# Score matmuls of an attention layer in quarters of the TensorE array, two rounds at a time

## The chip, the cores and the metric

One core of a Trainium2 chip runs the kernel; the other seven have nothing to do. The metric is the time of one execution on the device, in microseconds (us). Instructions run on TensorE (matmuls, PE in the rows; its weight loads PEld), VectorE (DVE), ScalarE (ACT) and GpSimd (POOL); SyncE (SP) issues most of the DMAs.

## What is computed

An attention layer with a causal window of 128 positions and a distance bias, over 4 batches of 8 heads of 64 with 576 positions, and behind it two feed-forward layers over its 2304 tokens:

```python
scores = scale * np.matmul(q, k.transpose(0, 1, 3, 2))
bias = slopes[:, None, None] * (-np.abs(rel).astype(np.float32))[None, :, :]
mask = (rel >= 0) & (rel < window)
scores = np.where(mask, scores + bias[None], -1000000000.0)
...
attn = attn / (np.sum(attn, axis=-1, keepdims=True) + 1e-09)
out = np.matmul(attn, v)
...
x = ((x @ w_a) * (x @ w_b)) @ w_out      # 512 -> 1536 -> 512
return bent(x @ w_in2) @ w_out2          # 512 -> 2048 -> 512
```

The weights are 64-bit floats; the kernel turns each slice of 128 columns or rows into a high and a low 32-bit part ("decodes" it) before it is used.

## The kernel before

**Attention.** Two heads are worked on together, as a pair `hp`: their 64 dimensions each fill the 128 partitions. A batch has nine blocks of 64 queries; each sees its own 64 keys and the 128 before, so that a block of scores has up to 192 columns (64 and 128 for the first two). Two blocks are a round (`m`, five rounds for batches 1 to 3, the last with one block). A unit is a batch, a pair of heads and a part of the rounds; batch 0 has eight units in two parts, the other batches four each.

`scores` (L315) works on a round. One matmul a block (L327) gives the 64 queries of both heads at once: its left operand is a block of `diag`, 128x128, that holds q of the first head in the upper left quarter, q of the second in the lower right, and zeros elsewhere. q and k of batches 1 to 3 come in from DMA as 32x32 pieces and are transposed by VectorE in `prep_unit` (L300, two half transposes of q into the diagonal of `diag`; L303, k). Scores and bias are added by VectorE, which takes the maximum in the same pass (L333), ScalarE does the exponential (L337), GpSimd and VectorE the reciprocal of the sum (L342, L343), and GpSimd and ScalarE the scaling (L346, L348). Three rounds later `transposes` turns the probabilities by matmuls with the identity (L359), a copy brings them back, and five rounds later `values` multiplies them with v (L391), a unit at a time, with 64x64 and 128x64 tiles; the product goes to a pair `xh`, `xl` (L153, L147). All matmuls of attention are of plain 32-bit floats, and each leaves two records in the trace, a transposing one leaves one.

PSUM: `ps_at` has four banks for scores (one per round), transposes (one) and value products (two).

**Feed-forward.** `gate` and `down1` run up and down products (L540 to L542, then L613, L641 to L643 and L679 to L681) with high and low parts in three matmuls each. The first 1536 tokens are taken in half blocks of 256 as soon as their attention is done; these run interleaved with attention, a step of attention after every one or two steps of products (`PACE`). The first half block needs twelve decoded weights one after the other, the second finds them there. Decoding takes five or six VectorE passes over 128x512 (L491 to L499), GpSimd's sums (L505, L147) and ScalarE's copies (L489, L506).

**Order.** The Python code emits instructions in this interleaved order; a scheduler with a model of the engines then sets the order on each engine, which is fixed in the program. Each engine runs its list strictly in that order, waiting on semaphores.

Of the kernel before, what the change touches and what calls it, by code (L numbers as in the profile page):

```python
# [9 lines left out]
F32 = mybir.dt.float32  # L10
# [4 lines left out]
ALU = mybir.AluOpType  # L15
# [11 lines left out]
def attention_and_two_ffns(  # L27
# [59 lines left out]
    SB = 4  # L87
# [82 lines left out]

    biases = []
    for hp in range(NPAIR):
        bias = att.tile([P, 3 * D], F32, tag=f"bias{hp}", name=f"bias{hp}", bufs=1)
        for j in range(2):
            nc.vector.tensor_scalar(
                bias[j * D : (j + 1) * D], rel[j * D : (j + 1) * D],
                -(2.0 ** (-8.0 * (2 * hp + j + 1) / H)) / QSCALE, NEG / QSCALE,
                ALU.mult, ALU.max,
            )
        biases.append(bias)  # L180
    diag = []
    for z in range(NDIAG):
        t = att.tile([P, NQ, P], F32, tag=f"diag{z}", name=f"diag{z}", bufs=1)
        nc.vector.memset(t, 0.0)
        diag.append(t)

# [100 lines left out]
    def prep_unit(u):  # L287
        b, part, hp = units[u]
        if b == 0:
            turn_start(part, hp, diag[u % NDIAG])  # L290
            if (part, hp) == (1, NPAIR - 1):
                retired.update(("first", z) for z in range(5))
            return
        q0, q1, k0 = PART[part]
        qr, kr = prep[b, part, hp]
        qd = diag[u % NDIAG]
        kt = att.tile([P, NK], F32, tag="kt", name="kt")
        for j in range(2):
            me = slice(j * D, (j + 1) * D)
            nc.vector.transpose(  # L300
                qd[me, : (q1 - q0) // D, me], qr[me].rearrange("p (n t) -> p n t", t=D)
            )
        nc.vector.transpose(kt[:, : q1 - k0], kr)  # L303
        prep[b, part, hp] = (qd, kt)

    def qblocks(m):
        return [i for i in (2 * m, 2 * m + 1) if i < S // D]
# [4 lines left out]
    rounds = {}  # L312
    values_of = {}

    def scores(b, hp, m):  # L315
        part = part_of(b, m)
        q0, _, k0 = PART[part]
        qd, kt = prep[b, part, hp]
        ps = ps_at.tile([P, 2, 4 * D], F32, tag="at", name="ps_s")
        count["t"] += 1  # L320
        s_sb = probs[count["t"] % SB]
        at = lambda z, i: s_sb[:, z, first_col(i) :]
        nmax = att.tile([P, 2], F32, tag="nmax", name="nmax", bufs=6)
        ssum = att.tile([P, 2], F32, tag="ssum", name="ssum", bufs=6)
        for z, i in enumerate(qblocks(m)):
            c = first_col(i)
            nc.tensor.matmul(  # L327
                ps[:, z, c : 3 * D], qd[:, i - q0 // D, :],
                kt[:, (i - 2) * D + c - k0 : (i + 1) * D - k0], start=True, stop=True,
            )  # L330
        for z, i in enumerate(qblocks(m)):
            cs = slice(first_col(i), 3 * D)
            nc.vector.tensor_tensor_reduce(  # L333
                at(z, i), ps[:, z, cs], biases[hp][:, cs], -QSCALE, BIG,
                ALU.add, ALU.min, nmax[:, z : z + 1],
            )
            nc.scalar.activation(  # L337
                at(z, i), at(z, i), AF.Exp,
                bias=nmax[:, z : z + 1], scale=-1.0, accum_out=ssum[:, z : z + 1],
            )  # L340
        n = len(qblocks(m))
        nc.gpsimd.tensor_scalar(ssum[:, :n], ssum[:, :n], 1e-9, 1.0, ALU.add, ALU.mult)  # L342
        nc.vector.reciprocal(ssum[:, :n], ssum[:, :n])  # L343
        for z, i in enumerate(qblocks(m)):
            if E_N[2 * b + (m >= 2)][z] == "A":
                nc.scalar.activation(at(z, i), at(z, i), AF.Copy, scale=ssum[:, z : z + 1])  # L346
                continue
            ENG[E_N[2 * b + (m >= 2)][z]].tensor_scalar(  # L348
                at(z, i), at(z, i), ssum[:, z : z + 1], 1.0, ALU.mult, ALU.mult
            )  # L350
        rounds[b, hp, m] = s_sb
# [12 lines left out]
    def values(b, hp, part):  # L364

        q0, _, _ = PART[part]
        vt = values_of[b, part, hp]
        ms = ROUNDS_OF[part]  # L370
        pts = {m: rounds.pop((b, hp, m)) for m in ms}
        po = [ps_at.tile([P, TB], F32, tag="at", name="ps_o") for _ in range(2)]
        todo_ = []
        for m in ms:
            todo_ += [(0, m, slice(0, D), vt, m, 1, j) for j in range(2)]
            if m > 0 and len(qblocks(m)) == 2:
                todo_ += [(1, m, slice(D, P), vt, m - 1, 1, j) for j in range(2)]
        for m in ms:
            if m > 0:
                todo_ += [(0, m, slice(0, P), vt, m - 1, 0, j) for j in range(2)]  # L380
            if len(qblocks(m)) == 2:
                todo_ += [(1, m, slice(0, P), vt, m, 2, j) for j in range(2)]
        seen = set()
        left = {}
        for z, m, _, _, _, _, j in todo_:
            left[z, m, j] = left.get((z, m, j), 0) + 1
        for z, m, rows, vt, n, u, j in todo_:
            me = slice(j * D, (j + 1) * D)
            left[z, m, j] -= 1
            c = (m - ms[0]) * D  # L390
            nc.tensor.matmul(  # L391
                po[z][me, c : c + D], vt(n, j)[rows], pts[m][rows, u, me],
                start=(z, j) not in seen, stop=left[z, m, j] == 0, skip_group_check=True,
            )
            seen.add((z, j))
        for z in range(2):
            mine = [m for m in ms if z < len(qblocks(m))]
            tok = lambda m: b * S + (2 * m + z) * D
            for i in sorted({tok(m) // TB for m in mine}):
                those = [m for m in mine if tok(m) // TB == i]  # L400
                c, n0 = (those[0] - ms[0]) * D, (tok(those[0]) - blocks[i][0]) // D
                src = po[z][:, c : c + len(those) * D].rearrange("p (n t) -> p n t", t=D)
                xh, xl = (
                    x[:, hp].rearrange("p (n t) -> p n t", t=D)[:, n0 : n0 + 2 * len(those) - 1 : 2]
                    for x in xs[i]
                )
                ecopy(E_X[2 * b + int(part == 1)], xh, src)
                minus(nc.vector, xl, src, xh)
# [7 lines left out]
    ]  # L416
    done = set()

    def attention():
        load_start()  # L420
        prep_unit(0)
        seen = -1
        for n in range(len(todo) + LV):
            if n < len(todo):
                u, t = todo[n]
                if u != seen:
                    seen = u
                    if u + 1 < len(units):
                        prep_unit(u + 1)
                    if u + AHEAD < len(units):  # L430
                        load_unit(*units[u + AHEAD])
                    values_of[units[u]] = load_values(*units[u])
                scores(*t)
                yield
            if 0 <= n - LT < len(todo):
                transposes(*todo[n - LT][1])
# [367 lines left out]
```

## Time and profile before

| | |
|---|---|
| median of 3 runs | 995.21 us (995.11 to 998.65) |
| the profiled execution | 996.27 us |
| its span, first to last instruction | 994.4 us |
| mean granted TensorE clock | 0.992 of full |
| busy: TensorE matmuls, weight loads | 969.7, 842.4 us |
| busy: VectorE, ScalarE, GpSimd | 609.7, 407.2, 177.7 us |

Busy time of TensorE counts every moment at which a matmul is under way; matmuls overlap, so the sum of their lengths is longer, and the step from one start to the next says more than a length. Shares over the whole span are averages over stages with different limits, so the trace is read by windows below.

### The profile page before, as it was taken

How to read it: one execution, taken by the hardware profiler on the slowest of the kernel's cores; microseconds unless marked ns; L12 is line 12 of the kernel's file. 1: busy time of each engine (PE TensorE's matmuls, PEld its weight loads, DVE VectorE, ACT ScalarE, POOL GpSimd, SP SyncE). 2: the span in 40 equal slices, each digit the busy share in tenths (PEclk: the TensorE clock that was granted, in tenths of full speed). 3: DMA queues.
4: the chain of work that ended last, by engine and by line, in shares of the span. 5: the costliest groups of instructions: out<-in, count | busy, mean ns of one | idle time of the engine just before them, and what ended most of it. 6: DMA issues, size and time to landing. Idle time of an engine off the chain costs nothing.

```text
span 994.4 us, 15931 instructions
## 1 busy us (share of the span) xinstructions
PE 969.7 (98%) x6052; PEld 842.4 (85%) x6052; DVE 609.7 (61%) x1366; ACT 407.2 (41%) x998; POOL 177.7 (18%) x285
## 2 busy tenths in 40 slices
PE   5997999999999999999999999999999999999998
PEld 4876999999989888888988888888888888888887
DVE  6699855553616993223995299635995446644443
ACT  5887677663214441112342245333552223322222
POOL 5567633331101100000212224000020000000001
PEclk9999999999999999999999999999999999999999
DMA  9756444213311331000331023100230000001111
GB/s 208 146 122 147 110 87 74 57 35 133 113 53 45 125 106 43 0 1 1 105 91 60 1 63 85 44 1 1 85 107 22 1 1 21 1 1 43 43 43 63
DMA packets 115403, 61.83 MB, mean 62 GB/s; under 512 B 87040, under 2 KB 107520, under 8 KB 114944
## 3 DMA queue, kind: packets, MB, share of 16 engines
q1 hardware_dynamic: 113184, 60.31, 22.7%
q8 instruction: 47, 0.77, 0.3%
q10 hardware_dynamic: 2144, 0.52, 0.2%
q14 instruction: 28, 0.23, 0.1%
HBM read 52.95 MB, written 7.86 MB: 61 GB/s over the span
## 4 chain that ended last, share of the span: by engine, by line
PE 87%; DVE 3%; DMA 1%; issue 1%; ACT 0%; POOL 0%; DVEq 0%; POOLq 0%; SPq 0%; ACTq 0%
PE mm L540 16%; PE mm L541 16%; PE mm L542 16%; PE acc L681 7%; PE acc L679 7%; PE acc L680 7%; PE acc L613 4%; PE acc L643 3%; PE acc L642 3%; PE acc L641 3%; PE ps_s L327 3%; PE ps_o L391 2%; PE ps_t L359 1%; DMA w<-in_moe_w_out_dram 1%; DVE e L499 0%
## 5 line engine op out<-in xcount | busy, mean ns | idle before, releaser
L540 PE MATMUL mm<-xh,wh 128*128 128x512 f32 (+1 forms) x912 | 318.6, 350 | 0.0
L541 PE MATMUL mm<-xl,wh 128*128 128x512 f32 (+1 forms) x912 | 315.6, 346 | 0.0
L542 PE MATMUL mm<-xh,wl 128*128 128x512 f32 (+1 forms) x912 | 315.0, 346 | 0.1
L540 PEld LDWEIGHTS mm<-xh,wh 128*128 128x128 f32 x912 | 173.0, 190 | 21.6
L541 PEld LDWEIGHTS mm<-xl,wh 128*128 128x128 f32 x912 | 173.1, 190 | 21.1
L542 PEld LDWEIGHTS mm<-xh,wl 128*128 128x128 f32 x912 | 172.8, 189 | 21.3 <-POOL wl L147 0.4
L596 ACT ACTIVATE c_sb<-c_sb,half 128x512 f32<-128x512 f32 (+1 forms) x80 | 54.5, 681 | 165.6 <-DVE c_sb L595 165.6
L585 DVE TENSOR_TENSOR a_sb<-mm,a_sb 128x256 f32<-128x256 f32 (+1 forms) x74 | 40.1, 542 | 121.1 <-PE mm L542 114.0
L679 PE MATMUL acc<-wh,gh 128*128 128x512 f32 x288 | 112.3, 390 | 0.2 <-ACT gh L562 0.2
L680 PE MATMUL acc<-wl,gh 128*128 128x512 f32 x288 | 112.2, 389 | 0.0
L681 PE MATMUL acc<-wh,gl 128*128 128x512 f32 x288 | 110.4, 390 | 0.3 <-POOL gl L147 0.3
L595 DVE TENSOR_SCALAR c_sb<-mm 128x512 f32<-128x512 f32 (+1 forms) x80 | 50.8, 636 | 81.9 <-PE mm L542 79.0
L147 POOL TENSOR_TENSOR gl<-c_sb,gh 128x256 fp32r<-128x256 f32 x16 | 15.6, 974 | 384.1 <-ACT gh L562 374.2
L147 POOL TENSOR_TENSOR gl<-a_sb,gh 128x256 fp32r<-128x256 f32 x40 | 35.4, 886 | 255.6 <-ACT gh L562 255.0
L597 DVE SCALAR_TENSOR_TENSOR c_sb<-mm,c_sb 128x512 f32<-128x512 f32 (+1 forms) x80 | 50.7, 635 | 39.0 <-ACT c_sb L596 39.0
L580 ACT COPY a_sb<-mm 128x256 f32<-128x256 f32 (+1 forms) x74 | 34.4, 464 | 89.2 <-PE mm L542 89.0
L562 ACT CAST gh<-a_sb 128x256 fp32r<-128x256 f32 (+1 forms) x74 | 37.2, 503 | 82.0 <-DVE a_sb L585 81.7
L562 ACT CAST gh<-c_sb 128x512 fp32r<-128x512 f32 (+1 forms) x80 | 46.2, 579 | 55.9 <-DVE c_sb L597 47.7
L506 ACT CAST wh<-e 128x512 fp32r<-128x512 f32 x68 | 42.2, 621 | 63.1 <-DVE e L505 38.2
L489 ACT ACTIVATE e<-w 128x512 f32<-128x512 f32 x65 | 43.8, 673 | 56.8 <-DVE wl L147 13.9
L642 PE MATMUL acc<-gl,wh 128*128 128x512 f32 (+1 forms) x184 | 66.3, 362 | 0.2 <-DVE gl L147 0.2
L337 ACT ACTIVATE s<-s,nmax 128x192 f32<-128x192 f32 (+2 forms) x144 | 62.0, 433 | 9.9 <-DVE nmax L333 9.5
(77 smaller groups left out, 1614.8 us busy)
## 6 DMA issues: line engine op xcount, KB each, us to landing
w<-in_moe_w_out_dram SPq DMA_DIRECT2D x28, 512.0 KB, 3.6
w<-in_moe_w_in_dram SPq DMA_DIRECT2D x16, 512.0 KB, 3.6
w<-in_moe_w_a_dram SPq DMA_DIRECT2D x12, 512.0 KB, 3.8
w<-in_moe_w_b_dram SPq DMA_DIRECT2D x12, 512.0 KB, 3.7
out_dram<-osum SPq DMA_DIRECT2D x18, 256.0 KB, 2.1
qraw<-in_q_dram SPq DMA_DIRECT2D x48, 72.0 KB, 2.8
kraw<-in_k_dram SPq DMA_DIRECT2D x48, 72.0 KB, 2.8
v<-in_v_dram SPq DMA_DIRECT2D x25, 128.0 KB, 2.8
```

The source lines that it names most:

```text
L147: eng.tensor_tensor(out_, a, hi.bitcast(F32), ALU.subtract)
L337: nc.scalar.activation(at(z, i), at(z, i), AF.Exp, bias=nmax[:, z : z + 1], scale=-1.0, accum_out=ssum[:, z : z + 1],)
L540: nc.tensor.matmul(ps, wh[:, cs], xh[:, c], start=(c == 0), stop=False)
L541: nc.tensor.matmul(ps, wh[:, cs], xl[:, c], start=False, stop=False)
L542: nc.tensor.matmul(ps, wl[:, cs], xh[:, c], start=False, stop=(c == NC - 1))
L562: nc.scalar.copy(hi[:, :n], t[:, :n])
L595: nc.vector.tensor_scalar(c_sb[:, :n], ph[:, :n], -1.0, None, ALU.max)
L596: nc.scalar.activation(c_sb[:, :n], c_sb[:, :n], AF.Square, bias=half, scale=0.5)
L642: nc.tensor.matmul(accs[c][:, :n], wh[:, cs], gl, start=False, stop=False)
L679: nc.tensor.matmul(accs[s], gh[:, ss], wh, start=begin, stop=False)
L680: nc.tensor.matmul(accs[s], gh[:, ss], wl, start=False, stop=False)
L681: nc.tensor.matmul(accs[s], gl[:, ss], wh, start=False, stop=end)
```

## The change

For batches 1 to 3 `diag` and its zeros go. q is transposed like k, in one pass over 128 partitions, into `qt`. `scores_two` takes two rounds that follow each other (also from one unit into the next) and two banks. A block becomes two matmuls of 64 rows by 64 columns of the array, one per head: head j's q and k lie on partitions 64j and up, so it uses row half j; the first block of a round writes to bank 0 with head j at partitions 64j, the second to bank 1 with the heads swapped. So the four matmuls of a round use four different quarters of the array. VectorE and ScalarE work on the two rounds one after the other as before; the bias has a second copy with the heads swapped, and `values` reads the turned probabilities from the other half. The next unit is prepared behind the scores that open a unit, not ahead of them. Batch 0 keeps `diag`, which is now five blocks long instead of nine.

```diff
-        bias = att.tile([P, 3 * D], F32, tag=f"bias{hp}", name=f"bias{hp}", bufs=1)
+        bias = att.tile([P, 2, 3 * D], F32, tag=f"bias{hp}", name=f"bias{hp}", bufs=1)
+        for y in range(2):
+            for j in range(2):
+                me = slice((j ^ y) * D, ((j ^ y) + 1) * D)
+                nc.vector.tensor_scalar(
+                    bias[me, y], rel[me],
...
-        t = att.tile([P, NQ, P], F32, tag=f"diag{z}", name=f"diag{z}", bufs=1)
+        t = att.tile([P, NQ - 4, P], F32, tag=f"diag{z}", name=f"diag{z}", bufs=1)
...
-        for j in range(2):
-            me = slice(j * D, (j + 1) * D)
-            nc.vector.transpose(
-                qd[me, : (q1 - q0) // D, me], qr[me].rearrange("p (n t) -> p n t", t=D)
-            )
+        nc.vector.transpose(qt[:, : q1 - q0], qr)
         nc.vector.transpose(kt[:, : q1 - k0], kr)
...
+    def scores_two(two):
+        banks = [ps_at.tile([P, 2, 4 * D], F32, tag="at", name="ps_s") for _ in range(2)]
+        for y, (b, hp, m) in enumerate(two):
+            qt, kt = prep[b, 2, hp]
+            for z, i in enumerate(qblocks(m)):
+                c = first_col(i)
+                for j in range(2):
+                    me, to = (slice(h * D, (h + 1) * D) for h in (j, j ^ z))
+                    nc.tensor.matmul(
+                        banks[z][to, y, c : 3 * D], qt[me, i * D : (i + 1) * D],
+                        kt[me, (i - 2) * D + c : (i + 1) * D], start=True, stop=True,
+                        skip_group_check=True,
+                    )
+        return [[bank[:, y] for bank in banks] for y in range(2)]
...
-                at(z, i), ps[:, z, cs], biases[hp][:, cs], -QSCALE, BIG,
+                at(z, i), ps[z][:, cs], biases[hp][:, z if b else 0, cs], -QSCALE, BIG,
...
+            turned = slice((j ^ z) * D, ((j ^ z) + 1) * D) if b else me
...
-                po[z][me, c : c + D], vt(n, j)[rows], pts[m][rows, u, me],
+                po[z][me, c : c + D], vt(n, j)[rows], pts[m][rows, u, turned],
...
-                scores(*t)
+                if t[0] == 0:
+                    if u != seen:
+                        begin(u)
+                        seen = u
+                    scores(*t, scores_one(*t))
+                else:
+                    if n % 2 == 0:
+                        banks = scores_two([r for _, r in todo[n : n + 2]])
+                    scores(*t, banks[n % 2])
+                    if u != seen and (n % 2 or todo[n + 1][0] == u):
+                        begin(u)
+                        seen = u
```

The order that the scheduler makes of it differs, on TensorE above all. In the rows a name is a tile with its number, `mm` and `acc` are products of the feed-forward layers, `ps_s`, `ps_t`, `ps_o` scores, transposes and value products, and the size is that of the output. First, two wide rounds of the first pair of heads of batch 2 on TensorE, before:

```order
L542 MATMUL mm_1923<-xh0_106,wl_1161 128x256
L327 MATMUL ps_s_1898<-kt_1650,diag0_128 128x192 x2
L359 MATMUL ps_t_1917<-ident_84,s3_138 128x128 x3
L327 MATMUL ps_s_1927<-kt_1650,diag0_128 128x192 x2
L359 MATMUL ps_t_1943<-ident_84,s0_132 128x128 x2
L540 MATMUL mm_1969<-xh0_106,wh_1254 128x256
```

and after the change:

```order
L575 MATMUL mm_2172<-xh1_108,wl_243 128x256
L339 MATMUL ps_s_1975<-kt_1701,qt_1700 64x192 x2
L339 MATMUL ps_s_1976<-kt_1701,qt_1700 64x192 x2
L339 MATMUL ps_s_1975<-kt_1701,qt_1700 64x192 x2
L339 MATMUL ps_s_1976<-kt_1701,qt_1700 64x192 x2
L380 MATMUL ps_t_1998<-ident_84,s0_140 128x128 x2
```

Two rounds with a bank each, four matmuls on the whole array, became one stretch of eight on quarters, with tiles of another shape in front of it and behind it.

Second, two wide rounds of the next pair of heads on TensorE, after the change:

```order
L413 MATMUL ps_o_2061<-pt_1969,v2_150 64x64 x2
L380 MATMUL ps_t_2143<-ident_84,s3_146 128x128 x3
L339 MATMUL ps_s_2152<-kt_1916,qt_1915 64x192 x4
L573 MATMUL mm_2172<-xh1_108,wh_242 128x256
L573 MATMUL mm_2203<-xh1_108,wh_293 128x256
L574 MATMUL mm_2172<-xl1_109,wh_242 128x256
L575 MATMUL mm_2172<-xh1_108,wl_243 128x256
L574 MATMUL mm_2203<-xl1_109,wh_293 128x256
L575 MATMUL mm_2203<-xh1_108,wl_294 128x256
L339 MATMUL ps_s_2153<-kt_1916,qt_1915 64x192 x4
L380 MATMUL ps_t_2176<-ident_84,s0_140 128x128 x3
```

Here the four matmuls on bank 0 (`ps_s_2152`) and the four on bank 1 (`ps_s_2153`) stand apart, with six products on the whole array between them.

Third, VectorE between its last passes on two weights (`w64_1143` is the ninth, `w64_1158` the tenth that is decoded), before:

```order
L499 SCALAR_TENSOR_TENSOR e_1147<-w64_1143,e_1147 128x512
L333 ISA s1_134,nmax_1337<-ps_s_1336,bias1_119 128x192
L333 ISA nmax_1337 128x1
L333 ISA s1_134,nmax_1337<-ps_s_1336,bias1_119 128x192
L333 ISA nmax_1337 128x1
L343 RECIPROCAL ssum_1281<-ssum_1281 128x2
L585 TENSOR_TENSOR a_sb_1022<-mm_1024,a_sb_1022 128x256
L492 TENSOR_SCALAR e_1162<-e_1162 128x512
L333 ISA s2_136,nmax_1362<-ps_s_1361,bias1_119 128x192
L333 ISA nmax_1362 128x1
L300 STREAM_TRANSPOSE diag1_130<-qraw_1223 64x9x64 x2
L303 STREAM_TRANSPOSE kt_1427<-kraw_1228 128x576
```

and the stretch behind the ninth weight's last pass after the change:

```order
L532 SCALAR_TENSOR_TENSOR e_1169<-w64_1165,e_1169 128x512
L147 TENSOR_TENSOR xl1_109<-ps_o_1207,xh1_108 128x64
L354 ISA s3_146,nmax_1308<-ps_s_1299,bias1_121 128x192
L354 ISA nmax_1308 128x1
L525 TENSOR_SCALAR e_1184<-e_1184 128x512
L528 TENSOR_SCALAR e_1184<-e_1184 128x512
L618 TENSOR_TENSOR a_sb_1034<-mm_1036,a_sb_1034 128x256
L354 ISA s0_140,nmax_1338<-ps_s_1298,bias1_121 128x192
L354 ISA nmax_1338 128x1
L529 SCALAR_TENSOR_TENSOR up_1185<-w64_1180,e_1184 128x512
```

The transposes of q and k that stood between the two weights are not there; the next ones (one of q, one of k) follow behind the tenth weight's last pass.

## Rows read from the trace of the kernel before

**Rows 1.** The page, busy time of each engine, share of the span, instructions:

```profile
PE 969.7 (98%) x6052; PEld 842.4 (85%) x6052; DVE 609.7 (61%) x1366; ACT 407.2 (41%) x998; POOL 177.7 (18%) x285
```

**Rows 2.** Windows: busy us (instructions) of each engine, granted clock, DMA share, GB/s:

```profile
25.40:50.00 24.60, 24.09 (x245) 21.24 (x246) 16.83 (x67) 21.54 (x76) 13.09 (x25) 0.93 0.73 143
50.00:99.70 49.70, 42.32 (x451) 36.17 (x451) 48.66 (x155) 39.51 (x135) 36.35 (x56) 0.95 0.64 135
99.70:102.50 2.80, 2.80 (x19) 2.61 (x18) 1.65 (x2) 0.26 (x1) 1.39 (x1) 0.63 0.73 118
102.50:227.10 124.60, 124.60 (x1434) 121.59 (x1432) 75.60 (x307) 86.66 (x313) 50.19 (x114) 1.00 0.31 70
```

**Rows 3.** Timeline of VectorE, 88 to 96 us: start, length, line, operation, tiles:

```profile
88.84 0.35 DVE L333 CUSTOM_DVE_ANT_0 s<-ps_s,bias 128x192 f32<-128x192 f32 x1
...
89.12 0.21 DVE L147 TENSOR_TENSOR xl<-ps_o,xh 128x64 fp32r<-128x64 f32 x1
89.25 1.53 DVE L496 SCALAR_TENSOR_TENSOR up<-w,e 128x512 uint32<-128x512 uint32 x1
...
92.22 0.68 DVE L499 SCALAR_TENSOR_TENSOR e<-w,e 128x512 f32<-128x512 uint32 x1
...
93.33 0.77 DVE L300 STREAM_TRANSPOSE diag<-qraw 64x576 f32<-64x576 f32 x1
94.03 0.56 DVE L492 TENSOR_SCALAR e<-e 128x512 f32<-128x512 f32 x1
```

**Rows 4.** Timeline of TensorE, 92 to 103.5 us; in brackets the idle time before:

```profile
94.93 0.47 PE L359 MATMUL ps_t<-ident,s 128*128 128x128 f32 x1 [2.47 <-POOL s L348]
...
99.69 0.41 PE L540 MATMUL mm<-xh,wh 128*128 128x256 f32 x1
...
102.51 0.71 PE L327 MATMUL ps_s<-kt,diag 128*128 128x64 f32 x4
102.98 0.36 PE L542 MATMUL mm<-xh,wl 128*128 128x256 f32 x1
```

**Rows 5.** Timeline of TensorE, 137 to 139 us:

```profile
137.15 0.81 PE L327 MATMUL ps_s<-kt,diag 128*128 128x192 f32 x4
137.80 0.49 PE L359 MATMUL ps_t<-ident,s 128*128 128x128 f32 x3
```

**Rows 6.** Groups by line and shape, TensorE: count, busy us, mean ns of one:

```profile
L327 PE MATMUL ps_s<-kt,diag 128*128 128x192 f32 x224 | 50.5, 344 | 2.2 <-DVE nmax L333 1.4 <-DVE xl L147 0.9
L327 PE MATMUL ps_s<-kt,diag 128*128 128x64 f32 x32 | 6.7, 295 | 1.2 <-DVE kt L155 0.8 <-DVE xl L147 0.4
```

**Rows 7.** Windows of L391 alone: matmuls, weight loads, clock, DMA:

```profile
131.59:132.32 0.73, 0.73 (x32) 0.66 (x33) 1.00 0.00 0
132.32:133.40 1.08, 1.08 (x36) 1.01 (x32) 1.00 0.30 56
```

**Rows 8.** Timeline of TensorE, 116.6 to 117.6 us:

```profile
116.68 0.28 PE L541 MATMUL mm<-xl,wh 128*128 128x256 f32 x1
116.80 0.28 PE L542 MATMUL mm<-xh,wl 128*128 128x256 f32 x1
117.01 0.32 PE L391 MATMUL ps_o<-pt,v 64*64 64x64 f32 x2
117.26 0.39 PE L613 MATMUL acc<-gh,wh 128*128 128x256 f32 x1
117.49 0.28 PE L613 MATMUL acc<-gl,wh 128*128 128x256 f32 x1
```

**Rows 9.** Groups by line, VectorE, to 240 us:

```profile
L300 DVE STREAM_TRANSPOSE diag<-qraw 64x576 f32<-64x576 f32 x24 | 18.5, 770 | 0.4
...
L184 DVE MEMSET diag<- 128x1152 f32 x2 | 2.0, 1018 | 0.4 <-issue 0.4
...
L175 DVE TENSOR_SCALAR bias<-rel 64x192 f32<-64x192 f32 x8 | 1.8, 252 | 0.0
```

**Rows 10.** Timeline of SP's queue, 0 to 60 us:

```profile
23.29 4.33 SPq L254 DMA_DIRECT2D qraw<-in_q_dram  x4
```

More of the change, by code (lines that the diff above doesn't have):

```diff
@@ L172, in attention_and_two_ffns @@
     for hp in range(NPAIR):
-        bias = att.tile([P, 3 * D], F32, tag=f"bias{hp}", name=f"bias{hp}", bufs=1)
-        for j in range(2):
[L175 to L178, printed above, removed]
-            )
+        bias = att.tile([P, 2, 3 * D], F32, tag=f"bias{hp}", name=f"bias{hp}", bufs=1)
[4 more added lines that the diff above has]
+                    bias[me, y], rel[me],
+                    -(2.0 ** (-8.0 * (2 * hp + j + 1) / H)) / QSCALE, NEG / QSCALE,
+                    ALU.mult, ALU.max,
+                )
         biases.append(bias)
@@ L295, in prep_unit @@
         qr, kr = prep[b, part, hp]
-        qd = diag[u % NDIAG]
+        qt = att.tile([P, NK], F32, tag="qt", name="qt")
         kt = att.tile([P, NK], F32, tag="kt", name="kt")
-        for j in range(2):
-            me = slice(j * D, (j + 1) * D)
-            nc.vector.transpose(
-                qd[me, : (q1 - q0) // D, me], qr[me].rearrange("p (n t) -> p n t", t=D)
-            )
+        nc.vector.transpose(qt[:, : q1 - q0], qr)
         nc.vector.transpose(kt[:, : q1 - k0], kr)
-        prep[b, part, hp] = (qd, kt)
+        prep[b, part, hp] = (qt, kt)
     def qblocks(m):
@@ L313, in attention_and_two_ffns, with scores_one @@
     values_of = {}
-    def scores(b, hp, m):
+    def scores_one(b, hp, m):
         part = part_of(b, m)
@@ L319, in scores @@
         ps = ps_at.tile([P, 2, 4 * D], F32, tag="at", name="ps_s")
[L320 to L324, printed above, removed]
         for z, i in enumerate(qblocks(m)):
@@ L330, in scores @@
             )
+        return [ps[:, z] for z in range(2)]
+    def scores_two(two):
[10 more added lines that the diff above has]
+                        skip_group_check=True,
+                    )
+        return [[bank[:, y] for bank in banks] for y in range(2)]
+    def scores(b, hp, m, ps):
+        count["t"] += 1
+        s_sb = probs[count["t"] % SB]
+        at = lambda z, i: s_sb[:, z, first_col(i) :]
+        nmax = att.tile([P, 2], F32, tag="nmax", name="nmax", bufs=5)
+        ssum = att.tile([P, 2], F32, tag="ssum", name="ssum", bufs=5)
         for z, i in enumerate(qblocks(m)):
@@ L417, in attention_and_two_ffns, with begin @@
     done = set()
+    def begin(u):
+        if u + 1 < len(units):
+            prep_unit(u + 1)
+        if u + AHEAD < len(units):
+            load_unit(*units[u + AHEAD])
+        values_of[units[u]] = load_values(*units[u])
     def attention():
@@ L425, in attention @@
                 u, t = todo[n]
[L426 to L432, printed above, removed]
-                scores(*t)
+                if t[0] == 0:
[10 more added lines that the diff above has]
+                        seen = u
                 yield
```

## The prediction

> **What bounds the kernel now.** I read the busy shares first: TensorE's matmuls are busy for 969.7 us, 98% of the span [rows 1]. A busy TensorE need not be at its peak, so next come the windows, split where the work changes [rows 2]. From 102.5 us on TensorE is busy without a gap at full clock, while VectorE has 75.6 of 124.6 us of work: there the end is set by TensorE's own work, and what another engine saves is worth nothing. From 50.0 to 99.7 us it is the other way: VectorE is busy 48.66 of 49.70 us, TensorE 42.32, and the granted clock averages 0.95. From 25.4 to 50 us VectorE has 16.83 of 24.60 us.
>
> The end of that starved stretch is seen in the timelines. VectorE finishes the last pass on the eleventh weight (L499) at 92.22 + 0.68 us [rows 3]. TensorE then waits 2.47 us for GpSimd's normalised scores, restarts at 94.93, and at 99.69 begins the second half block of tokens, whose weights are all decoded [rows 4]. I call that moment M. After it TensorE is never short of work. Between 99.70 and 102.50 us the clock averages 0.63 of full [rows 2]: TensorE had stood idle, and part of that stretch ran at 1.2 instead of 2.4 GHz. So a sum has two parts: when M comes, and how much TensorE work is left after M.
>
> **Prices on TensorE.** A score block of 128x192 leaves two records; two blocks take 137.80 - 137.15 = 0.65 us, or 0.326 each [rows 5]. That is 0.163 per record, 0.85 ns per column. The narrow blocks of 64 and 128 columns: four records from 102.51 to 102.98 us [rows 4], about 0.45 after what the change of tile shape before them takes, 0.225 a block, because the 128-column weight load limits them. 112 blocks are wide and 32 narrow (224 records of the wide ones, two a block, 32 of those of 64 columns and as many of those of 128 [rows 6]): 36.5 + 7.2 = 43.7 us of scores. 28 wide and 8 narrow ones belong to batch 0 and stay.
>
> Do four quarters run at once? The value products show it. In two windows the same number of matmuls run, 16 and 16, with 32 records each [rows 7] (the 36 of the second count four that were still under way). On tiles of 128x64 two sit side by side, so they take 16 steps: 1.08 us. On 64x64 tiles (ten on the upper rows, six on the lower) they take 0.73. Had the two row halves taken turns, that would be 16 steps too. Ten steps of 0.054 (64 columns at 0.85 ns) and sixteen explain 0.54 and 0.87; the remainder, 0.19 and 0.21, is the change of tile shape. So both row halves and both column halves run together, each quarter as a queue of its own.
>
> What does a change of shape cost? A lone matmul on a 64x64 tile sits between 256-column ones: 116.80 to 117.49 us is 0.69, less two of 0.12 and its own two records of 0.054, leaves 0.34 for two changes, 0.17 each [rows 8]. The windows give up to 0.2, but there each of 10 and 16 steps has some overhead; with 4 ns a step they give 0.15. I take **0.16 us per change**, bounds 0.1 and 0.2.
>
> **The change on TensorE.** Of the 108 blocks of batches 1 to 3 each becomes two quarters. A run with both banks complete (two wide rounds) takes 4 records x 0.163 = 0.65 us instead of 1.30; a run of one round and half (three wide blocks) still 0.65 instead of 0.98, since one bank has two of them. But the program's order, in front of this, does not always keep a run together: the six pairs of rounds 1 and 2 in every second unit are cut by weight matmuls into a run on bank 0 and one on bank 1. Each of these uses two quarters only and takes 0.65, so such a pair saves nothing and pays four changes of shape. In all there are 38 runs: 10.9 us (batch 0) + 22.0 = 32.9 us of scores, 10.8 less than before. The value products are moved too: in six units all the upper-row products now stand before the lower-row ones with 128x64 ones between, which adds 17 steps of 0.116 (two records), 2.0 us. And changes of shape go from 89 to 167, counted along both orders: 78 x 0.16 = 12.5 us. The net on TensorE is -10.8 + 2.0 + 12.5 = **+3.7 us**: the change buys array time and pays more for switching.
>
> Only what lies after M counts in full. Counted along the two orders, after M:
> - scores: 24.6 us before (63 wide, 18 narrow); now 31 runs, 20 of 0.65, 4 of 0.54, 5 of 0.44, 2 of 0.22: 17.9;
> - transposes of 128x128: 125 before, 132 now, at 0.11: +0.8;
> - value products: 133 steps before, 160 now, at 0.116: +3.1;
> - weight products: +0.2, a few that stood before M or behind;
> - changes of shape: 36 before, 105 now: 69 x 0.16 = 11.0.
>
> Sum: -6.7 + 0.8 + 3.1 + 0.2 + 11.0 = **+8.4 us after M**. The rest of the net, 3.7 - 8.4 = -4.7, is ahead of M. Much of this is attention that stood before M and now stands behind it: VectorE's queue has fewer score blocks ahead of the same weight.
>
> **The change on VectorE, and M.** Each unit of batches 1 to 3 had two transposes of q at 0.77 us (24 in all, 64 partitions each [rows 9]); it now has one of 128 partitions and the same length, so 12 x 0.77 = 9.2 us go. Eight more bias rows at 0.25 and two memsets of 640 instead of 1152 columns (1.02 each) add 2.0 - 0.9 = 1.1 us at the start. Two q and one k transpose of the first units move ahead of the fifth weight, into the stretch where VectorE is idle a third of the time; the first waits for its loads, whose issue takes from 23.29 to 27.62 us [rows 10] and would be done about when VectorE comes to it. I let these cost 1 us before 50 us (bounds 0 and 3).
>
> Between the last passes on the fifth and on the eleventh weight VectorE's queue had 32 score blocks, 16 low parts of values, 8 q and 4 k transposes; it now has 23, 11, 2 and 3, and the same weight passes. Steps from one start to the next: a score block 0.28, a low part 0.13, a transpose 0.70 [rows 3]. So 9 x 0.28 + 5 x 0.13 + 7 x 0.70 = 8.1 us less. Because that stretch is VectorE's, M would come 8.1 us earlier less the 1 us, if no other engine takes over. ScalarE has 39.5 and GpSimd 36.4 of the 49.7 us [rows 2], part of it for the same score blocks, and both sit in the chain to M, so I take 7 of the 8.1: M comes **7 less 1 = 6 us earlier**; bounds 0 and 11 (rival 1). TensorE's own work ahead of M is 4.7 less too, so it does not stand against this. The half clock after M costs 0.37 x 2.8 = 1.0 us [rows 2]; it goes with the long wait, and I count it as gained (bounds 0 and 1).
>
> **Sum.** -6 - 1 + 8.4 = **+1.4 us**, on a span of 994.4 and 996.27 us for that execution. The median of the runs shown is 995.21, 1.1 lower, and I apply the difference to it: **996.6 us**. After the end of attention nothing changes: some 3,750 matmuls of the same kinds stand there in either order. DMAs are the same in number; ScalarE and GpSimd do the same work.
>
> **Rivals.**
> 1. *TensorE stays fed before M.* From 50 to 99.7 us TensorE stands idle for 49.70 - 42.32 = 7.4 us, and the clock takes 5%, 2.5 us [rows 2]. If relief removes two thirds of these 10 beside the 4.7 of work that is moved, M comes 11 us earlier: -11 - 1 + 8.4, 991.6; if all of them, 988. For it: VectorE at 98% and no other engine above 80%. Against: the wait at 94.93 was for GpSimd, in whose queue weights and scores alternate. Under 990.2 I give 0.15.
> 2. *The pair of banks becomes a wait.* Scores of two rounds now hold two of the four banks of `ps_at` until all four reductions (0.28 each) are done; transposes need one more and value products two. TensorE is served in order, so a run that finds its bank taken stops the weight matmuls behind it. Before, there is no such wait after M. At 31 runs, 0.3 us each gives +9: 1006; it makes the kernel slower by over 0.5% from 0.12 us per run on. The cuts in the pairs are places where the order itself makes room for this, which speaks for it. Chance 0.17.
> 3. *Quarters of one bank take turns.* In the value products the upper rows write one bank and the lower rows another (the windows of [rows 7] are of these); in the new scores upper and lower rows write the same bank at different partitions, which no row of before shows. If they took turns, the 17.9 us after M would double: 1014. I give 0.1, as the partitions differ. The Trainium skill, "TensorEngine Tiling (Array Packing)", section "Restrictions and Gotchas", says that row tiles cannot access one PSUM bank at the same time; taken to the letter this rival is its forecast, and no run shown tests it.
>
> The other 0.58 is the forecast's, with its own range 991 to 1002: 0.15 to 0.2 per change of shape is 3 us, M the rest.
>
> **Numbers.** This kernel's measurement can tell a difference of 0.5%, 5 us, from none. Faster by more: 0.15, rival 1 at its strong end. Slower by more (over 1000.2): rivals 2 and 3, 0.27, and the upper end of the forecast: 0.3. The same: 0.55. The range 988 to 1007 takes in rivals 1 and 2, and leaves out rival 3 and the extremes of 2.
>
> **What would show it.** Right: score runs of 0.65 us for eight quarters with four starting together; gaps of 0.15 to 0.2 us at both ends of each; 38 runs; VectorE's transposes halved; M at 91 to 96 us; the end of attention some 8 us further behind M. Wrong: runs of 1.3 us (rival 3), TensorE waiting for VectorE or ScalarE at scores or transposes after M (rival 2), M before 90 us (rival 1), or changes of shape that cost under 0.1 us.

## The result, and the profile after

The median went from 995.38 us (995.11 to 998.65) to **1002.06 us** (1001.57 to 1002.75): a ratio of 1.0065, 95% interval 1.0053 to 1.0077, so 6.7 us slower. The forecast was 996.6 with a range of 988 to 1007. The profiled execution, in which all that follows in this section is read, was the longest of the four: 1002.75 us, with a span of 1001.0 and a mean clock of 0.993 (the other three 0.996 to 0.997).

The page of the changed kernel [rows 1]:

```profile
PE 973.8 (97%) x6268; PEld 829.9 (83%) x6268; DVE 602.1 (60%) x1362; ACT 408.0 (41%) x998; POOL 176.2 (18%) x285
```

Windows of the changed kernel, cut at 50 us, at M (now 95.85 us), and at 113 us, a little behind TensorE's last wait, which ends at 110.70; columns as in [rows 2]:

```profile
25.40:50.00 24.60, 24.11 (x249) 20.53 (x251) 18.24 (x72) 22.09 (x79) 11.71 (x25) 1.00 0.84 166
50.00:95.85 45.85, 40.11 (x420) 31.69 (x418) 39.87 (x127) 33.19 (x114) 33.14 (x47) 0.85 0.56 116
95.85:113.00 17.15, 14.98 (x172) 12.98 (x170) 15.25 (x41) 11.63 (x37) 13.34 (x18) 1.00 0.58 141
113.00:239.50 126.50, 126.50 (x1633) 112.10 (x1630) 65.00 (x293) 85.14 (x307) 43.37 (x110) 1.00 0.28 59
```

and of the kernel before, from M (99.70) on:

```profile
99.70:113.00 13.30, 13.30 (x103) 13.05 (x103) 10.79 (x30) 8.40 (x29) 9.49 (x11) 0.92 0.54 139
113.00:125.00 12.00, 12.00 (x145) 11.51 (x144) 10.01 (x29) 7.41 (x25) 8.58 (x12) 1.00 0.38 78
```

Two things stand out. Ahead of M VectorE was busy for 48.66 of 49.70 us and is now busy for 39.87 of 45.85: the work went, and 6 us of idleness came. Behind M TensorE was never idle and now is for 17.15 - 14.98 = 2.17 us. The waits of TensorE from M to 113 us in the changed kernel say for whom (waiting line, whom for, us in total, times, longest):

```profile
PE ps_o L413 <- DVE nmax L354: 1.2, 1, 1.2
PE mm L573 <- DVE a_sb L618: 0.6, 1, 0.6
PE ps_s L339 <- ACT pt L153: 0.4, 1, 0.4
```

and those of VectorE from 50 us to M:

```profile
DVE s L354 <- PE ps_s L339: 3.5, 2, 2.8
DVE a_sb L618 <- PE mm L575: 0.7, 1, 0.7
```

VectorE now waits for scores from TensorE, 3.5 us, and TensorE for VectorE; both work through fixed lists. From 64 to 70 us TensorE was idle for 2.6 of 6 us, and from 68.95 to 82.60 us it ran at half clock, 1.2 GHz:

```profile
64.00:70.00 6.00, 3.38 (x32) 2.28 (x28) 5.81 (x18) 3.59 (x14) 4.70 (x8) 0.91 0.29 89
68.95:82.60 13.65, 12.81 (x92) 9.87 (x93) 9.04 (x33) 8.35 (x29) 7.02 (x12) 0.50 0.53 97
```

There VectorE was idle for 13.65 - 9.04 = 4.6 us, most of its 6. The longest wait for scores, by its timeline:

```profile
79.15 0.36 DVE L354 CUSTOM_DVE_ANT_0 s<-ps_s,bias 128x192 f32<-128x192 f32 x1 [2.77 <-PE ps_s L339]
```

So the clock took more ahead of M than before (a mean of 0.85 instead of 0.95 from 50 us to M) and less behind it.

The timeline of TensorE at M [rows 4] and about a whole run of scores [rows 5]:

```profile
95.27 0.41 PE L380 MATMUL ps_t<-ident,s 128*128 128x128 f32 x2 [0.63 <-DVE xl L147]
...
95.85 0.38 PE L573 MATMUL mm<-xh,wh 128*128 128x256 f32 x1
...
131.78 0.28 PE L575 MATMUL mm<-xh,wl 128*128 128x256 f32 x1
131.99 0.88 PE L339 MATMUL ps_s<-kt,qt 64*64 64x192 f32 x16
132.80 0.66 PE L380 MATMUL ps_t<-ident,s 128*128 128x128 f32 x4
```

The run of eight quarters (16 records) takes 132.80 - 131.99 = 0.81 us to the next start: 0.65 of scores and 0.16 for the change of shape behind them; ahead of it 0.21 instead of 0.12. The last passes on the fifth and the eleventh weight [rows 3], by VectorE's timeline:

```profile
52.07 0.68 DVE L532 SCALAR_TENSOR_TENSOR e<-w,e 128x512 f32<-128x512 uint32 x1
...
91.11 1.63 DVE L532 SCALAR_TENSOR_TENSOR e<-w,e 128x512 f32<-128x512 uint32 x1
```

Before, the fifth weight's came at 48.47:

```profile
48.47 1.11 DVE L499 SCALAR_TENSOR_TENSOR e<-w,e 128x512 f32<-128x512 uint32 x1
```

The last value product of attention starts at 239.29 us, before at 233.37; what follows takes 761.7 and 761.0 us. So the loss lies ahead of the end of attention: M 3.8 us earlier, and 143.4 instead of 133.7 us from M to there.

### The profile page after: what moved, and what is told of

It is laid out like the page before. It is cut to its first block, busy times and chain, and to the rows that moved or that the text cites. A ratio compares the mean times of both kernels' runs of the same rounds, so it can differ in the third digit from the quotient of the medians.

```text
span 1001.0 us, 16384 instructions
## 1 busy us (share of the span) xinstructions
PE 973.8 (97%) x6268; PEld 829.9 (83%) x6268; DVE 602.1 (60%) x1362; ACT 408.0 (41%) x998; POOL 176.2 (18%) x285
## 4 chain that ended last, share of the span: by engine, by line
PE 85%; DVE 4%; issue 1%; DMA 0%; ACT 0%; POOL 0%; DVEq 0%; SPq 0%; ACTq 0%
PE mm L573 15%; PE mm L574 15%; PE mm L575 15%; PE acc L713 6%; PE acc L712 6%; PE acc L714 6%; PE acc L646 4%; PE acc L675 3%; PE acc L676 3%; PE acc L674 3%; PE ps_o L413 2%; PE ps_s L339 2%; PE ps_t L380 2%; DVE up L529 0%; DVE e L528 0%
## 5 line engine op out<-in xcount | busy, mean ns | idle before, releaser
L629 ACT ACTIVATE c_sb<-c_sb,half 128x512 f32<-128x512 f32 (+1 forms) x80 | 54.5, 681 | 166.6 <-DVE c_sb L628 166.6
```

The lines of the kernel that those rows point to most:

```text
L629: nc.scalar.activation(c_sb[:, :n], c_sb[:, :n], AF.Square, bias=half, scale=0.5)
```

## The experiments

Times are medians; ratios are to the kernel before, with their 95% interval. M and the start of the last value product (E) are read in each profiled execution.

| | edit | us | ratio | M | E |
|---|---|---|---|---|---|
| | before | 995.4 | 1 | 99.69 | 233.37 |
| | changed | 1002.06 | 1.0065 (1.0053 to 1.0077) | 95.85 | 239.29 |
| e1 | before, relief alone | 993.68 | 0.9981 (0.9972 to 0.9991) | 92.86 | 230.94 |
| e2 | changed, relief undone | 1005.99 | 1.0108 (1.0093 to 1.0122) | 94.28 | 239.87 |
| e3 | pairs in a block | 1081.10 | 1.0860 (1.0845 to 1.0875) | 114.06 | 318.89 |
| e4 | bias rows by DMA | 1000.99 | 1.0059 (1.0046 to 1.0073) | 95.35 | 238.28 |
| e5 | pairs kept by an edge | 1009.09 | 1.0133 (1.0113 to 1.0154) | 99.24 | 243.62 |
| e6 | fewest visits | 1013.34 | 1.0176 (1.0150 to 1.0202) | 93.85 | 253.39 |
| e7 | before, lone quarters | 1050.66 | | | |
| e8 | before, two quarters | 1057.64 | | | |
| e9 | before, pair order alone | 999.65 | 1.0037 (1.0024 to 1.0050) | 98.67 | 235.27 |
| e10 | quarters in batch 1 only | 995.67 | 1.0001 (0.9992 to 1.0010) | 94.03 | 233.12 |
| e11 | quarters in batches 2, 3 only | 1004.24 | 1.0079 (1.0062 to 1.0096) | 100.17 | 243.26 |
| e12 | changed, lighter weights | 999.01 | 1.0038 (1.0025 to 1.0051) | 93.50 | 235.56 |

e7 and e8 are one run each, the others 4 to 12. In e2 and e3 ten weight products that stand behind M elsewhere stand ahead of it.

**e1 and e2: relief with and without quarters.** In e1 (kernel before) the loop over the halves of q is cut to one, in e2 (changed kernel) the pass is done twice:

```diff
-        for j in range(2):
+        for j in range(1):
...
-        nc.vector.transpose(qt[:, : q1 - q0], qr)
+        for _ in range(2):
+            nc.vector.transpose(qt[:, : q1 - q0], qr)
```

> The kernel before with one of its two q transposes a unit (12 of 0.77 us fewer on VectorE, 9.2 us in all, no extra bias rows; the q of every odd head in batches 1 to 3 is left out). Relief theory: what the change gains comes from VectorE alone, so M comes 4 to 6 us earlier here too, some 3 us of attention moves behind M by the two orders, and the time is 990 to 994. Rival (the relief is worth nothing, since ScalarE, GpSimd and the chain of one round set M): M within 1 us of before, 994 to 996.

> The changed kernel with its q transpose done twice (12 more of 0.77 us on VectorE, as many as before the change). Relief theory: M goes back by 4 to 5 us, to about 100, and the time is 1005 to 1007, which is the price of the quarters alone (plus 9 to 12 on before). Rival (VectorE has room, the transposes are hidden): M at 96, time 1001.5 to 1003.

Relief alone brings M 6.8 us earlier, and the time falls by 1.9 us only: from M to E it is 4.4 us more, 3.0 of it attention that stood ahead of M and now stands behind (forecast from the orders); the other 1.4 is not accounted for. Undone in the changed kernel it costs 4.3 us (1.0108 against 1.0065). So relief is worth 2 to 4 us and the rest of the change costs 8.4 to 10.8. The expected late M of e2 was not seen: M came at 94.28, but TensorE then stood idle for 18.72 - 16.05 = 2.7 us until 113:

```profile
94.28:113.00 18.72, 16.05 (x189) 14.53 (x187) 17.93 (x43) 11.70 (x38) 13.51 (x16) 0.91 0.32 99
```

M is not the end of the starved stretch, as I had taken it to be. The profiled execution of e2 was its shortest, 1003.1 us at a mean clock of 0.996; the other three had 0.991 and took 1005.35 to 1007.45, while the changed kernel took 1001.96 and 1002.16 at 0.996. So most of what the undone relief costs goes with TensorE's half clock.

**e3 and e5: cut pairs made whole.** In e3 the eight quarters stand in an indivisible block, in e5 an edge holds back the first quarters of the six cut pairs until the second bank is free (the first two lines are of e3, the rest of e5):

```diff
+        with tc.tile_critical():
+            for y, (b, hp, m) in enumerate(two):
...
+                    if two[0][2] == 1 and y == z == 0:
+                        after(mm, "low")
...
-                minus(nc.vector, xl, src, xh)
+                last["low"] = minus(nc.vector, xl, src, xh).ins
```

> The changed kernel with the eight quarters of a pair of rounds kept together in the order (30 score runs instead of 38, no pair cut by weight products). Shape theory: eight runs of 0.65 us or less and some four to ten changes of shape of 0.15 go, 5.4 us less on TensorE by the two orders, 3.2 of it after M: 997 to 999. Rival (the cut pairs were room for the banks; kept whole, TensorE waits for VectorE at each run): 1002 to 1008, with waits of TensorE at the score line of over 0.3 us each after M.

> The changed kernel with one edge added for the six cut pairs: their first quarter is issued only once VectorE has made the low part of the values before it, which frees the second bank; nothing else waits. 31 score runs instead of 38. Shape theory: TensorE has 5.9 us less work up to the end of attention by the two orders, and the time falls by 4 to 6 us: 996 to 998. Rival (the waits matter, not the shapes; a run that holds two banks stops TensorE whatever its order): 1001 to 1004.

e3 tells nothing of the shapes. Its waits of TensorE from 113 to 240 us show scores waiting for loads of v, which they don't read; the block waits for more than its operands, and the mean clock fell to 0.957:

```profile
PE ps_s L340 <- DMA v<-in_v_dram: 10.0, 3, 4.1
PE ps_s L340 <- DMA kraw<-in_k_dram: 8.0, 3, 3.6
```

e5 has only the edge, and both theories missed: 1009.1. Between M and E it has 40 weight products more (4.8 us at 0.12) and takes 0.9 us more, so 3.9 less for the same work, as the shape theory has it. This was given back twice. M is 3.4 us later than in the changed kernel; the waits of TensorE from 76 to 90 us have row reductions and ScalarE's `gh`:

```profile
PE ps_s L349 <- DVE nmax L366: 2.0, 1, 2.0
PE acc L658 <- ACT gh L607: 2.0, 1, 2.0
```

And behind E, by TensorE's timeline, it waits 4.5 us for the low part of the last values, while the 40 weight products that could have covered this stand ahead now:

```profile
248.43 0.55 PE L585 MATMUL mm<-xh,wh 128*128 128x256 f32 x1 [4.53 <-DVE xl L147]
```

Ahead of M the half clock came with it: TensorE was busy for 8.96 of the 14 us from 76 to 90, and from about 84 to 98 us it ran at 1.2 GHz, from 90 on without a gap, while VectorE was busy for 6.31 of 10 us:

```profile
90.00:100.00 10.00, 10.00 (x96) 8.86 (x94) 6.31 (x16) 3.54 (x11) 5.80 (x8) 0.60 0.44 77
```

Why an edge on so few pairs makes these waits is not settled.

**e4: the bias rows.** The swapped rows are copied by DMA:

```diff
-        for y in range(2):
-            for j in range(2):
...
+    def swap_biases():
+        for bias in biases:
+            for j in range(2):
+                nc.sync.dma_start(
+                    bias[(1 - j) * D : (2 - j) * D, 1], bias[j * D : (j + 1) * D, 0]
+                )
```

> The changed kernel with the swapped bias rows copied by eight DMAs instead of computed by VectorE (8 x 0.25 us fewer at the start). Start theory: the first weight's last pass comes 1.5 to 2 us earlier, the fifth's 1 to 2, M 1 to 2, and the time is 1000 to 1001. Rival (the start has slack, and the fifth weight is late for the first units' transposes): M within 0.5 us of the changed kernel's 95.9, time 1001.5 to 1002.5.

1.1 us by the medians, with intervals that overlap: no more than the 2.0 us of VectorE work, and perhaps less. The last pass on the fifth weight came 5.9 us earlier than in the changed kernel (52.07), far more than expected, and M only 0.5:

```profile
46.19 0.68 DVE L539 SCALAR_TENSOR_TENSOR e<-w,e 128x512 f32<-128x512 uint32 x1
```

So M does not follow the fifth weight; from 50 to 64 us VectorE was now idle for 3.4 us.

**e6: everything that saves a change of shape**, e4 and e5 with the products of a unit kept whole and turned around:

```diff
+        if b:
+            todo_ = todo_[::-1]
...
+            if b and not seen:
+                after(mm, "red")
```

> As e5, and the value products of a unit are kept whole too (an edge from the last row reduction to their first; 64x64 products last, next to a run of scores), and the swapped bias rows come by DMA as in e4. By the two orders TensorE has 11.6 us less work up to the end of attention than in the changed kernel and changes its shape 132 times instead of 166. Shape theory: 989 to 994, faster than the kernel before. Rival (what the quarters cost is waiting ahead of M, not work): 998 to 1001, no better than e4 by more than 3.

The order with the least work on TensorE took 1013.3 us, more than any other form of the change but e3. Its mean clock was 0.980 to 0.988; at 0.980 of 1014.7 us that is 20 us short of full speed, against 7 in the changed kernel. TensorE waits at the longer runs, as these lines for 113 to 260 us show:

```profile
PE ps_s L355 <- DVE xl L147: 3.8, 1, 3.8
PE ps_s L355 <- DVE nmax L372: 3.8, 2, 2.6
PE mm L596 <- DVE xl L147: 2.8, 1, 2.8
```

**e7 and e8: the price by itself.** In the last stage, `two` being 1 or 2:

```diff
+        if later:
+            wh, xh = weight(("i", f))[0], x[0]
+            for j in range(two):
+                me = slice(j * 64, j * 64 + 64)
+                nc.tensor.matmul(ph[me, :192], wh[me, me].bitcast(F32), xh[me, 0, :192].bitcast(F32), start=True, stop=True, skip_group_check=True)
```

> The kernel before with 80 lone quarters in its last stage, where TensorE waits for nothing: one fp32 product of 64x64 and 192 columns ahead of each first product of that stage, into a bank that the next product overwrites. Price theory: 0.33 us for the quarter and two changes of 0.15 each: 80 x 0.63 = 50 us, 1045 to 1047. Rival (a change is hidden by the loads of weights, and the gaps in the changed kernel are waits): 26 us, 1021 to 1023.

> As e7, with two quarters at each visit, on the upper and on the lower rows, into the upper and lower partitions of the same bank. If they run at once: the same time as e7 within 2 us. If quarters of one bank take turns: 80 x 0.33 = 26 us more than e7.

The 80 visits of e7 add 54.5 us to the span, 0.68 each, somewhat more than the 0.63 of the expectation; less the quarter's 0.33 that is 0.18 per change. In e8 the scheduler put other products between the two quarters at 11 places, so it has 91 visits; 61.5 us more are 0.68 each again. The two quarters of one visit take as long as one: four records in the 0.54 of two, with the next start 0.46 and 0.47 us behind. TensorE's timeline of e7:

```profile
699.85 0.54 PE L595 MATMUL mm<-xh,wh 64*64 64x192 f32 x2
700.31 0.50 PE L540 MATMUL mm<-xh,wh 128*128 128x512 f32 x1
700.65 0.39 PE L541 MATMUL mm<-xl,wh 128*128 128x512 f32 x1
```

and of e8:

```profile
701.13 0.54 PE L595 MATMUL mm<-xh,wh 64*64 64x192 f32 x4
701.60 0.50 PE L540 MATMUL mm<-xh,wh 128*128 128x512 f32 x1
```

**e9: the pair order alone**, with the blocks, `diag` and bias of the kernel before (against the changed kernel, `QB` being empty):

```diff
-                        banks = scores_two([r for _, r in todo[n : n + 2]])
+                        two = [r for _, r in todo[n : n + 2]]
+                        banks = scores_two(two) if t[0] in QB else [scores_one(*r) for r in two]
```

As in the changed kernel, `begin` stands behind the scores for batches 1 to 3, and the row maxima and sums have five buffers instead of six; that was not tried by itself, but in the trace of e9 VectorE's waits at the reductions are all for TensorE.

> The kernel before with the scores of two rounds of batches 1 to 3 issued together, as the change does, but still as 128x128 blocks: no quarters, no relief, no extra changes of shape. By the two orders TensorE's work is the same within 0.4 us. Shape theory (the loss of the change is the quarters' shapes and the order of the values): 995 to 996.5. Rival (the loss is in taking two rounds at a time, which holds two banks and gives VectorE four row reductions at once): 998 to 1002, with TensorE idle 3 to 5 us more up to 113 us than the 20 of before.

3.7 us slower with the same work (996.1 to 1002.1 over twelve executions). Not in the place that was expected: up to 113 us it has 21 idle us of TensorE to 20 before. It is between 113 and 125 us, where the kernel before kept TensorE busy at full clock, that the window shows e9 to lose 1.6 us idle and, at 0.86, another 1.4:

```profile
113.00:125.00 12.00, 10.36 (x114) 9.48 (x113) 8.87 (x27) 6.43 (x22) 9.31 (x12) 0.86 0.42 83
```

There TensorE waits 1.3 us for VectorE's copy of `y`, which frees the sums of a half block. In VectorE's timeline of e9 the transposes of the next unit, prepared behind the first scores of a pair, stand ahead of it:

```profile
114.07 0.97 DVE L537 TENSOR_SCALAR e<-e 128x512 uint32<-128x512 uint32 x1
114.96 1.57 DVE L307 STREAM_TRANSPOSE diag<-qraw 64x576 f32<-64x576 f32 x2
116.56 0.78 DVE L310 STREAM_TRANSPOSE kt<-kraw 128x576 f32<-128x576 f32 x1
117.26 0.65 DVE L155 COPY y<-acc 128x512 f32<-128x512 f32 x1
```

and in the kernel before behind it:

```profile
115.53 0.81 DVE L495 TENSOR_SCALAR e<-e 128x512 uint32<-128x512 uint32 x1
116.26 0.68 DVE L155 COPY y<-acc 128x512 f32<-128x512 f32 x1
...
117.13 1.57 DVE L300 STREAM_TRANSPOSE diag<-qraw 64x576 f32<-64x576 f32 x2
```

So the pair order costs by what it moves on a VectorE that is still nearly full (busy 9.73 of the 10 us from 110 to 120). Which part of it does this at other places, two rounds at once or the later `begin`, was not tried apart.

**e10 and e11: the quarters by batch.** `QB` is (1,) in e10 and (2, 3) in e11, with two half transposes into `diag` for the other batches and e4's bias rows (`PB` is empty; in e10 GpSimd also puts zeros back into `diag` for batch 2):

```diff
-            turned = slice((j ^ z) * D, ((j ^ z) + 1) * D) if b else me
+            turned = slice((j ^ z) * D, ((j ^ z) + 1) * D) if b in QB else me
...
-                if t[0] == 0:
+                if t[0] not in QB and t[0] not in PB:
```

> Quarters for batch 1 alone (12 score runs, of which 9 stand ahead of M), batches 2 and 3 as in the kernel before; swapped bias rows by DMA. Relief and shape theory: M 3 to 4 us earlier, 3.8 us more TensorE work behind it by the two orders: 994 to 996. Rival (the quarters cost their time ahead of M, in waits): 999 to 1002, with more TensorE idle time up to 113 us than before.

> Quarters for batches 2 and 3 alone (24 score runs, all behind M), batch 1 as in the kernel before; swapped bias rows by DMA. TensorE has 2.5 us more work behind M by the two orders, little relief ahead of it. Shape theory: 996.5 to 998.5. Rival (the quarters cost their time ahead of M): 995 to 996. Rival (behind M they cost more than their shapes, through the banks): over 1000.

Batch 1 alone: M 5.7 us earlier, more than expected; E and time the same, as the theory said. Batches 2 and 3 alone: 7.9 us more, where the orders give TensorE 2.5 us more work behind M. The time of the last rival came out: in the window of e9's loss TensorE is idle for 2.8 us, and at 0.83:

```profile
113.00:125.00 12.00, 9.22 (x95) 8.15 (x95) 9.85 (x23) 7.38 (x22) 9.39 (x13) 0.83 0.36 84
```

Its mechanism, the banks of the scores, hardly shows: TensorE's longest waits from 100 to 140 us are of products, for VectorE:

```profile
PE mm L593 <- DVE a_sb L638: 1.8, 1, 1.8
PE acc L666 <- DVE y L155: 0.7, 1, 0.7
```

**e12: is TensorE short of VectorE's work behind M?**

```diff
-        nc.vector.tensor_scalar(
+        if n not in range(11, 15):
+            nc.vector.tensor_scalar(
...
-        nc.vector.tensor_scalar(e, e, 5, 2, ALU.logical_shift_left, ALU.logical_shift_right)
+            nc.vector.tensor_scalar(e, e, 5, 2, ALU.logical_shift_left, ALU.logical_shift_right)
```

> The changed kernel with two of VectorE's six passes left out on the twelfth to fifteenth weight (8 passes, 5.4 us in the changed kernel's trace, all behind the eleventh weight; the bounds and the exponent shift of these four weights are left out); the order on TensorE stays as it was within 0.4 us of work. Theory (behind M TensorE still waits for VectorE until about 113 us): 2 to 3 us less, 999 to 1000.5, and TensorE's 2.2 idle us from 100 to 113 shrink to under 1. Rival (behind M TensorE is never short of work, as I forecast; what M came too late by is all ahead of it): 1001.5 to 1002.5.

3.0 us less, as the theory said, and not by the clock: at the same mean of 0.993 the changed kernel took 1002.75 us and e12 1000.2. From 100 to 113 us the idle time falls from 13 - 10.84 = 2.16 us to 0.42. The window of the changed kernel:

```profile
100.00:113.00 13.00, 10.84 (x130) 9.32 (x129) 12.54 (x32) 8.86 (x29) 9.67 (x13) 1.00 0.57 128
```

and of e12:

```profile
100.00:113.00 13.00, 12.58 (x147) 11.01 (x149) 10.68 (x29) 9.00 (x27) 11.04 (x14) 1.00 0.63 150
```

M was 2.4 us earlier as well, and from M to E it is 1.4 us less, so not all of the 3.0 lies behind M. Part of that is the clock. Up to the eleventh weight's last pass VectorE and TensorE of e12 run the same instructions in the same order as in the changed kernel, within 0.1 us of each other up to 67 us. Then the half clock lasted 3.4 us in e12's profiled execution and 13.65 in the changed kernel's, and that pass started 2.7 us earlier, at 88.39 instead of 91.11:

```profile
88.39 1.63 DVE L533 SCALAR_TENSOR_TENSOR e<-w,e 128x512 f32<-128x512 uint32 x1
```

No version beats both kernels: e1 is the only one below 995.4, and it leaves q of the odd heads out.

## Why the prediction was right or wrong

The range held, the size did not: +1.4 us forecast, +6.7 measured, at the upper end of the forecast's own 991 to 1002. Of the three outcomes it named, the likeliest (0.55, within 0.5%) did not come; "slower by more", with 0.3, did. That the range held is owed in part to its width: it was drawn to take in rivals 1 and 2, and neither set the time. By its steps:

- *Four quarters run at once; a run of eight takes 0.65 us.* Right: 0.81 with one change. Rival 3 fell, in the trace and in e8.
- *A change of shape costs 0.16 us.* Right in sum. A run of scores pays 0.09 us ahead of it and 0.16 behind; in e7 the second product behind a quarter starts late too (0.34 instead of 0.23 us after the first). The two changes of a visit are 0.35 us there, 0.18 each.
- *+8.4 us of TensorE work behind M.* Right: M to E grew by 9.8. Take off the 2.2 of waits that are new, and add 1.0 that the half clock took there before and that is gone (I had gained it in a term of its own): 8.6. That is what is left over, but its largest parts are in the trace as counted: 31 of the 38 runs of scores behind M, and 104 changes of shape from M to E, 35 before.
- *M comes 6 us earlier.* **The first step that failed**: 3.8, within the bounds of 0 and 11. Its parts: the last pass on the fifth weight starts at 52.07 instead of 48.47, 3.6 later (I had 1, bounds 0 and 3); from there to the eleventh it is 39.0 instead of 43.75, 4.7 less (I had 7); from there to M 2.7 less, which I had not counted. VectorE's work fell as counted: busy 8.8 us less from 50 us to M. But 98% busy became 87%, and of what was saved 3.5 us went into waits for scores. I had made the time a sum of VectorE's work, and let only ScalarE and GpSimd stand against it; the link that took over was TensorE's own list, above all at half clock. (Rival 1 had "no other engine above 80%" beside VectorE; TensorE, with 42.32 of 49.70 us, was at 85%.) How much the half clock cost is partly chance: where it lasted 3.4 us instead of 13.65, in e12, the eleventh weight's last pass came 2.7 us earlier behind the same lists, and M 6.2 us earlier than in the kernel before, with two VectorE passes less in front of it. The one execution in which M was read is the slowest of four and the one with the lowest mean clock; where M lay in the other three, which took 0.6 to 1.2 us less, is not known. And e4, where the fifth weight came 5.9 us earlier and M 0.5, shows that the three parts are not three causes.
- *"After M TensorE is never short of work."* True of the kernel before, and carried over to the changed one without a check: **the second step that failed**, 2.2 us of waits up to 113 us. e12 shows that VectorE's weight passes are behind a good part of them.
- *Rival 2, the pair of banks becomes a wait*: put at 0.3 us on each of 31 runs, 9 in all. The trace of the changed kernel shows it twice, for 1.6 us of the 2.2 behind M: a value product waits 1.2 us for row reductions and a run of scores 0.4 us for ScalarE's copy of transposed probabilities, and neither reads what it waits for, so it is the bank. Behind 113 us there is no wait at all. The pair order as a whole costs 3.7 us in e9, without a single quarter, but the wait there is for a copy behind moved transposes, not for a bank of scores. e5 and e6, where a run does wait for its banks, lose far more.
- *After the end of attention nothing changes.* 0.7 us of 761.

The sum, in the measured terms: -3.8 (M) - 1.0 (half clock) + 8.6 (work) + 2.2 (waits) + 0.7 (rest) = 6.7, the difference of the two spans being 6.6. It closes by construction, as the 8.6 is what the others leave.

Seen by its parts, the change buys 2 to 4 us of relief (e1, e2) and pays 3.7 for the pair order (e9), about 3 for shapes and split value products (counted in the orders at 0.15 a change) and up to 1 for bias rows (e4). The 3 are counted and not measured: no run has the quarters without the pair order. The parts don't add up exactly: e10 and e11, with e4's bias rows, give 0 and 7.9 where e4 gives 5.9. It may be that what a batch loses depends on the relief that the batches ahead of it have given; no run shows it.

## What to carry to other kernels

Counting removed work gives the gain only while the engine that loses it stays full: after the change, look for the engine that will wait next, its own feeder included. An order that issues work in larger lots moves other engines' work as well, and where the receiving engine is nearly full this can cost as much as the operations themselves. A stretch that was saturated before is so after the change only if the work arrives as early as it did. And idleness of TensorE can cost more than itself: behind 2.6 idle us it ran for 13.65 us at half clock here, and the engine that had been relieved waited for it.

## What of the hardware was not expected

**VectorE beside GpSimd.** A VectorE pass over 128x512 with one input (L525, L528, L530) takes 0.41 us in many places and up to 1.5 in others. In the changed kernel L528 took 1.39 us while GpSimd worked on 128x512 words:

```profile
111.46 0.40 DVE L525 TENSOR_SCALAR e<-e 128x512 f32<-128x512 f32 x1
111.54 1.45 POOL L538 TENSOR_TENSOR e<-up,e 128x512 f32<-128x512 f32 x1 [0.99 <-DVE ssum L364]
111.89 1.39 DVE L528 TENSOR_SCALAR e<-e 128x512 uint32<-128x512 uint32 x1
```

L525, which began before GpSimd's operation, took its 0.40 us; L528, which began behind it, ended 0.29 us behind its end. Of the 204 passes on these three lines 31 took over 0.6 us, and each of the 31 ended 0.28 or 0.29 us behind the end of a GpSimd operation that had begun before it. So "busy" of VectorE holds waits for GpSimd that no row calls a wait. The Trainium skill, "SBUF — State Buffer", "Summary: rules for kernel authors", says that where VectorE is in a 2-port mode, or has two SBUF inputs while GpSimd's operation reads SBUF, the second to issue blocks until the first is done. The rows agree with the order of issue; in which mode L528 ran they do not show.

**The length of a half clock.** In the changed kernel and in e12 TensorE was busy for the same 3.38 of the 6 us from 64 to 70. Then it ran at 1.2 GHz for 13.65 us in the one profiled execution and for 3.4 in the other. So a moment read behind such a stretch, like M, moves from one execution to the next.

**One bank, two row halves.** The Trainium skill, "TensorEngine Tiling (Array Packing)", "Restrictions and Gotchas", has it that row tiles cannot access one PSUM bank at once. For different partitions of the bank e8 shows otherwise: two quarters in the time of one.
